# Where a run-time branch stands in the start of an attention and mixer kernel, and which queue issues the first loads

## The chip, the cores and the metric

One core of a Trainium2 chip. The time is device time in microseconds (us) of that core, given as the median of several runs. A profile is one execution of the program taken by the hardware profiler; its times count from the start of its span. The engines are TensorE (PE; its weight loads are PEld), VectorE (DVE), ScalarE (ACT), GpSimd (POOL) and SyncE (SP). SP computes nothing: it issues DMAs. ACT and POOL can issue DMAs as well. A name with a q behind it (SPq, DVEq) is an engine's sequencer, which handles register loads, branches and DMA issues.

## The reference

Attention with root-mean-square norm on Q and K, 8 batches of 12 heads, 448 tokens of 64 values, and then an MLP mixer over tokens and channels. All data is float32.

```python
q_n, k_n = (rmsnorm(q, g_q), rmsnorm(k, g_k))      # x / sqrt(mean(x*x) + 1e-6) * g
scores = scale * np.matmul(q_n, k_n.transpose(0, 1, 3, 2))
scores = scores - np.max(scores, axis=-1, keepdims=True)
attn = np.exp(scores)
attn = attn / (np.sum(attn, axis=-1, keepdims=True) + 1e-09)
attn_out = np.matmul(attn, v)                       # (8, 12, 448, 64)
x = attn_out.transpose(0, 2, 1, 3).reshape(8, 448, 768)
h = np.maximum(x.transpose(0, 2, 1) @ w_tok1, 0.0) @ w_tok2
u = x + h.transpose(0, 2, 1)
out = u + np.maximum(u @ w_ch1, 0.0) @ w_ch2
```

## The kernel before, in words

**The two arms.** The kernel decides at run time whether the exponentials need their row maximum taken off. From g_q and g_k it computes one flag, `large` (lines 1334 to 1337, four small DVE instructions). Line 1533 loads the flag into a register of every engine, and each engine branches by itself into one of two copies of `whole`: with `shifted` true the maximum is taken off, with `shifted` false it isn't. The profiled data goes to the second copy. An engine meets the branch where its own stream of instructions has it; nothing makes the engines branch together.

**What stands ahead of the branch.** The class `Start` (line 1299) issues the first loads and begins on the first heads. Heads are handled in pairs, 48 in all; pair 0 and 1 are heads 0 to 3 of batch 0. `load_qk(p)` (line 1390) takes the Q and K rows of a pair with four DMAs, two for Q and two for K, made by `loads` (line 1394, issued at line 1406) on the two queues that it is given. Ahead of the branch:

- SP issues Q of pairs 0 and 1, and then Q and K of pairs 2 and 3; ACT issues K of pairs 0 and 1.
- POOL issues four tiny loads of g (line 1341), makes the identity matrix and some constants, and has the small memset of `summand` (line 1379) for the two buffers of squares.
- ACT squares pairs 0 and 1 (`square`, line 1421, instructions of line 1429), in two halves each.
- DVE sums the squares (`reduce`, line 1435, instructions of line 1445), takes reciprocal square roots by a guess and three Newton steps (`roots`, `guess`, `newton`, lines 1448 to 1499) and scales the rows (`scale`, line 1490, instructions of line 1496). Between the two sums stands one small product on `g_t` (line 1365), which ACT uses later as the scale of a copy.

Then comes the branch, on DVE behind the scalings of pair 1 and on SP behind the last load of pair 3.

**What stands behind the branch.** `whole` (line 84) has its engine order written out by hand for TensorE, DVE, ACT and GpSimd. SP begins at line 1204: V of pairs 0 and 1 (`load_v`, line 404), and then in turn the weight chunks 0 to 4 (`weight_load`, line 205, DMAs of line 222), Q and K of pairs 4 and 5, and V of pairs 2 to 5. ACT squares pair 2 (line 1216), copies pair 0's transposed rows out of PSUM, squares pair 3 (line 1221) and copies pair 1's. PE transposes pairs 0 and 1 (`turn_qk`, line 419, transposes of line 429, copies of lines 435 and 437). DVE sums and roots pairs 2 and 3 and scales them (lines 1222 to 1228).

The steady part starts at line 1240: `att_items` gives the steps of attention and `weight_items` those of the weights, and `merge` interleaves both by estimated costs. In a step PE computes scores (line 455), ACT takes their exponential (line 459), and PE multiplies by V (line 528) and by ones for the row sums (line 508). In steps 1 and 2 of attention ACT squares pairs 4 and 5 between its exponentials; at the end of step 3 PE transposes pairs 2 and 3. Weights arrive as 64-bit numbers and are made float32 on the way: DVE's lines 345 to 350, ACT's line 356 and DVE's line 379. The tile `raw` that holds a chunk has five buffers, so load i + 2 waits for the last conversion of chunk i - 3. Score tiles and transposes share one pool of four PSUM buffers (`ps_S`).

Of the kernel before, what the change touches and what calls it, by code (L numbers as in the profile page):

```python
# [13 lines left out]
ALU = mybir.AluOpType  # L14
# [69 lines left out]
def whole(ctx, tc, shifted, pre, q, k, v, g_q, g_k, moe_w_tok1, moe_w_tok2, moe_w_ch1, moe_w_ch2, out):  # L84


    nc = tc.nc
# [3 lines left out]
    B, H, S, D = q.shape  # L91
# [58 lines left out]
    ws2 = dram.tile([P, NF9 * 8, P], F32, name="ws2")  # L150

    st = dict(pre.st)
    m_tile = lambda: ps_M.tile([P, 512], F32, name="m_ps", tag="M")
    s_tile = lambda name: ps_S.tile([P, 512], F32, name=name, tag="S")

# [43 lines left out]
    def columns(i):  # L199
        return WCOLS if chunks[i][2] is None else chunks[i][2].shape[-1]  # L200

    def raw_tile():
        return raw_pool.tile([P, WCOLS, 2], U32, name="raw")

    def weight_load(i):
        rows, srcs, dst = chunks[i]
        wide = srcs[0].dtype == I64
        t = raw_tile()
        flat = t[0:rows].rearrange("p n w -> p (n w)")
        if not wide:  # L210
            t = t[:].rearrange("p n w -> p (n w)").bitcast(F32)
            flat = t[0:rows]
        n = columns(i) // len(srcs) * (1 + wide)
        for k, src in enumerate(srcs):
            to = flat[:, k * n:(k + 1) * n]
            for a, part in enumerate(src if isinstance(src, tuple) else (src,)):
                at = to[a * D:(a + 1) * D] if isinstance(src, tuple) else to
                if wide:
                    part = part.bitcast(U32)
                if len(part.shape) == 3:  # L220
                    at = at.rearrange("p (i n) -> p i n", i=part.shape[1])
                nc.sync.dma_start(out=at, in_=part)
        st["raw", i] = t
# [177 lines left out]
    def heads(p):  # L401
        return pre.heads(p)

    def load_v(p):
        b, hs = heads(p)
        st["v", p] = vt = pre.v_0 if p == 0 else st["v45"][:, p - 4, :] if p in (4, 5) else pre.v_t[p % 3]
        for a in range(2):
            nc.sync.dma_start(
                out=vt[rows_of(p, a)].rearrange("r (k d) -> r k d", d=D),
                in_=v[b, hs][a].rearrange("(k r) d -> r k d", r=D))  # L410

    def rows_of(p, a):

        return slice((a ^ p % 2) * D, (a ^ p % 2) * D + D)
# [788 lines left out]

    load_v(0)
    load_v(1)
    for i in range(5):
        weight_load(i)
        if i < 2:
            pre.load_qk(4 + i, st)
            load_v(2 + i)  # L1210

    st["v45"] = tu_pool.tile([P, 2, S], F32, name="v45", tag="tu")
# [86 lines left out]
class Start:  # L1299


    def __init__(self, ctx, tc, q, k, g_q, g_k, w2, g2, gate):
        self.nc = nc = tc.nc
        self.q, self.k = q, k
        B, H, S, D = q.shape
        self.NPAIR, self.NS, self.D = H // 2, 4, D
        self.R = S // self.NS
        P = 128
        pool = lambda name, bufs: ctx.enter_context(tc.tile_pool(name=name, bufs=bufs))
        const = pool("start", 1)  # L1310
        KF = w2.shape[0] // P // 2
        self.hb = const.tile([P, HB, 4, S // 2], F32, name="hb")

        flat = self.hb[:].rearrange("p q f s -> p (q f s)")
        n, o = 4 * self.NS * D, self.NPAIR * 4 * self.NS * D
        self.st = {("qk", p): flat[:, p * n:(p + 1) * n] for p in range(self.NPAIR)}
        self.qkT = [flat[:, o + i * 2 * S:o + (i + 1) * 2 * S].rearrange("p (i s) -> p i s", i=2) for i in range(3)]
        assert flat.shape[-1] >= o + 3 * 2 * S
        self.v_0 = const.tile([P, S], F32, name="v_first")[:]
        self.first_slot = self.NPAIR  # L1320
        self.far = 3 * self.NPAIR + 2
        qk_t = const.tile([P, 2, n], F32, name="qk_t")
        self.qk_t = [qk_t[:, i, :] for i in range(2)]
        self.v_t = [const.tile([P, S], F32, name=f"v_{i}")[:] for i in range(3)]

        warm = const.tile([P, 1], F32, name="warm")
        nc.vector.memset(warm[:], 1.0)
        self.load_qk(0, self.st, other=nc.scalar)
        self.load_qk(1, self.st, other=nc.scalar)
        nc.scalar.activation(out=warm[:], in_=warm[:], func=AF.Square)  # L1330
        gg = gate.tile([1, D], F32, name="gg")
        most = gate.tile([1, 1], F32, name="most")
        self.large = large = gate.tile([1, 1], I32, name="large")
        nc.vector.tensor_tensor(out=gg[:], in0=g2[:, 0, :], in1=g2[:, 1, :], op=ALU.mult)
        nc.vector.tensor_tensor(out=gg[:], in0=gg[:], in1=gg[:], op=ALU.mult)
        nc.vector.tensor_reduce(out=most[:], in_=gg[:], axis=AX_X, op=ALU.max)
        nc.vector.tensor_scalar(large[:], most[:], SCORE_BOUND**2 / D, None, ALU.is_gt)
        self.g_t = const.tile([P, 2], F32, name="g_t")
        for i, g in enumerate((g_q, g_k)):
            for a in range(2):  # L1340
                nc.gpsimd.dma_start(
                    out=self.g_t[a * D:(a + 1) * D, i:i + 1], in_=g.rearrange("(p o) -> p o", o=1))
        self.ident = const.tile([P, P], F32, name="ident")
        make_identity(nc, self.ident[:, :])
        self.one_c = const.tile([P, D], F32, name="one_c")
        nc.gpsimd.memset(self.one_c[:], 1.0)
        self.expo_c = const.tile([P, 1], F32, name="expo_c")
        nc.gpsimd.memset(self.expo_c[:], -896.0 * 2**23)
        self.sq = const.tile([P, 4 * self.NS, D + 1], F32, name="sq")


        self.sq_2 = flat[:, 0:4 * self.NS * (D + 1)].rearrange("p (r d) -> p r d", d=D + 1)
        self.sq_1 = qk_t[:].rearrange("p i n -> p (i n)")[:, 0:4 * self.NS * (D + 1)].rearrange(
            "p (r d) -> p r d", d=D + 1)
        for sq in (self.sq, self.sq_1):
            self.summand(sq)
        self.load_qk(2, self.st)
        self.load_qk(3, self.st)
        self.rs_0 = const.tile([P, 8 * self.NS], F32, name="rs_0")
        with tc.tile_pool(name="st_0", bufs=1) as self.st_pool:  # L1360
            self.nt_pool = self.st_pool
            for p in range(2):
                self.square(p, self.st)
            self.reduce(0, self.st)
            nc.vector.scalar_tensor_tensor(
                out=self.g_t[:, 0:1], in0=self.g_t[:, 0:1], scalar=float(D) ** 0.5, in1=self.g_t[:, 1:2],
                op0=ALU.mult, op1=ALU.mult)
            self.reduce(1, self.st)
            for part in self.roots(0, self.st):
                part()  # L1370
            for p in range(2):
                self.scale(p, self.st)

    def heads(self, p):
        b, j = divmod(p, self.NPAIR)
# [130 lines left out]
def kernel(  # L1506
# [26 lines left out]
    with tc.If(nc.values_load(large[0:1, 0:1], min_val=0, max_val=1,  # L1533
                              skip_runtime_bounds_check_because="a comparison's result") > 0) as arm:
        whole(tc, True, pre, *args)
    with arm.Else():
        whole(tc, False, pre, *args)
# [30 lines left out]
```

## Time and profile before

| | |
|---|---|
| median of 3 runs | 1285.12 us (1283.40 to 1287.99) |
| the profiled execution | 1283.78 us |
| its span | 1282.0 us |
| PE busy | 1251.6 us |
| DVE, ACT, POOL busy | 795.3, 393.3, 387.9 us |
| first transposes on PE | 12.77 us after the start |
| SP's last load ahead of the branch ends | 9.97 us |
| SP's first load behind the branch begins | 13.41 us |
| DMA, mean over the span | 178 GB/s |

The page first gives the busy time of each engine. A timeline line has start, duration, engine, source line, operation, what it writes and reads, and in square brackets how long the engine stood idle before it and what it waited for. A line of the view of waits has the instruction, the thing it waited for, the total in us, how often, and the longest. The DMA queues are q1 (SP), q10 (ACT), q0 (GpSimd) and two queues that carry instructions, q8 and q14.

### The profile page before, as it was taken

To read this page: it belongs to the slowest core of one execution; us is meant where nothing else is said; L and a number is where in the kernel's file an instruction comes from. 1 tells how busy PE (TensorE), PEld (TensorE's weight loads), DVE (VectorE), ACT (ScalarE), POOL (GpSimd) and SP (SyncE) were. 2 spreads that over 40 slices of the span, in tenths; PEclk is the share of its full clock that TensorE was granted. 3 is DMA by queue.
4 is the path that set the end of the run, shared out by engine and by line. 5 is a ranking of instruction groups with operands and counts; after the bars stand their busy time and mean duration, and the time that the engine had idled before them with its cause. 6 is when DMAs were issued, how large, how long until landed. Compare 5 with 4: busy or idle time off the path is not lost.

```text
span 1282.0 us, 20022 instructions
## 1 busy us (share of the span) xinstructions
PE 1251.6 (98%) x7236; PEld 890.8 (69%) x7236; DVE 795.3 (62%) x1241; ACT 393.3 (31%) x785; POOL 387.9 (30%) x629
## 2 busy tenths in 40 slices
PE   4999999999999999999999999999999999999998
PEld 3444444457744487796778768885887867797998
DVE  6989778856664255864668356765558456554243
ACT  5663433223341144302443033311343024300210
POOL 1202552024995611331133122241122322131222
PEclk9999999999999999999999999999999999999999
DMA  7866595899899876695657867595766864386554
GB/s 174 192 188 175 154 233 147 208 241 250 239 237 229 195 165 169 142 249 117 159 161 160 207 142 185 131 222 123 190 159 141 236 134 138 115 208 146 185 175 103
DMA packets 490112, 228.37 MB, mean 178 GB/s; under 512 B 371860, under 2 KB 450580, under 8 KB 490004
## 3 DMA queue, kind: packets, MB, share of 16 engines
q1 hardware_dynamic: 483394, 214.25, 67.9%
q0 software_dynamic: 3584, 12.06, 3.1%
q8 instruction: 59, 0.97, 0.3%
q10 hardware_dynamic: 3026, 0.69, 0.3%
q14 instruction: 49, 0.40, 0.1%
HBM read 184.26 MB, written 42.66 MB: 177 GB/s over the span
## 4 chain that ended last, share of the span: by engine, by line
PE 86%; DVE 6%; DMA 2%; SPq 2%; issue 1%; ACT 1%; DVEq 0%; ACTq 0%
PE m_ps L1001 26%; PE m_ps L1067 21%; PE s_ps L455 9%; PE o_ps L528 8%; PE m_ps L881 5%; PE m_ps L971 5%; PE m_ps L1050 4%; PE m_ps L839 2%; PE t_ps L839 2%; PE d_ps L508 1%; DVE raw L346 1%; DVE raw L348 1%; DVE stage L379 1%; DMA raw<-wp 1%; PE m_ps L846 1%
## 5 line engine op out<-in xcount | busy, mean ns | idle before, releaser
L1067 PE MATMUL m_ps<-hb,unit 128*128 128x224 f32 x1440 | 277.2, 354 | 0.0
L1067 PEld LDWEIGHTS m_ps<-hb,unit 128*128 128x128 f32 x1440 | 270.9, 190 | 8.8 <-issue 7.7
L1001 PE MATMUL m_ps<-tu,unit 128*128 128x224 f32 x1008 | 201.6, 355 | 1.3 <-ACT r L1011 1.3
L1001 PEld LDWEIGHTS m_ps<-tu,unit 128*128 128x128 f32 x1008 | 189.1, 190 | 15.1 <-issue 9.2
L459 ACT ACTIVATE e<-s_ps 128x448 f32<-128x448 f32 x294 | 138.1, 549 | 177.7 <-PE s_ps L455 169.4
L1001 PE MATMUL m_ps<-uT,unit 128*128 128x224 f32 x756 | 151.2, 354 | 0.5 <-DVE hb L1007 0.5
L1001 PEld LDWEIGHTS m_ps<-uT,unit 128*128 128x128 f32 x756 | 142.2, 190 | 7.6 <-issue 4.6
L455 PE MATMUL s_ps<-qkT 64*64 64x448 f32 x1260 | 143.7, 545 | 0.8 <-ACT x L821 0.8
L528 PE MATMUL o_ps<-e,v 64*64 64x448 f32 x1148 | 129.4, 538 | 0.3 <-ACT uT L565 0.2
L496 DVE TENSOR_TENSOR es<-es,e 128x896 f32<-128x896 f32 x90 | 103.5, 1150 | 13.0 <-ACT e L459 7.6
L1007 DVE TENSOR_TENSOR hb<-m_ps,r 128x448 f32<-128x448 f32 x63 | 39.1, 621 | 108.5 <-POOL r L1007 57.0
L1007 POOL TENSOR_TENSOR hb<-r,r 128x448 f32<-128x448 f32 x21 | 24.0, 1143 | 243.6 <-ACT r L1023 243.6
L455 PEld LDWEIGHTS s_ps<-qkT 64*64 64x64 f32 x1260 | 44.9, 132 | 70.0 <-issue 59.9
L528 PEld LDWEIGHTS o_ps<-e,v 64*64 64x64 f32 x1148 | 45.2, 133 | 62.9 <-issue 59.2
L1475 POOL TENSOR_TENSOR nt<-rs 128x56 f32<-128x56 f32 (+1 forms) x54 | 21.9, 405 | 203.5 <-DVE rs L1467 200.7
L1008 ACT ACTIVATE hb<-hb 128x448 f32<-128x448 f32 x84 | 48.4, 577 | 101.1 <-DVE hb L1007 77.6
L881 PE MATMUL m_ps<-w_sb,h 128*128 128x448 f32 x192 | 75.2, 544 | 0.3 <-DVE uT L886 0.3
L1082 POOL TENSOR_TENSOR uT<-uT,r 128x448 f32<-128x448 f32 x42 | 51.4, 1240 | 78.5 <-DVE r L1082 46.7
L320 POOL TENSOR_TENSOR raw<-raw 128x128 f32<-128x128 f32 x128 | 64.4, 522 | 34.3 <-DMA raw<-wp 29.8
L1445 DVE TENSOR_REDUCE ms<-sq 128x28 f32<-128x896 f32 (+2 forms) x44 | 47.5, 1080 | 35.6 <-ACT sq L1432 28.6
L1007 DVE TENSOR_TENSOR r<-m_ps,r 128x448 f32<-128x448 f32 x42 | 26.1, 622 | 64.3 <-PE m_ps L1001 64.3
L886 DVE TENSOR_TENSOR uT<-uT,m_ps 128x448 f32<-128x448 f32 x48 | 29.3, 613 | 54.5 <-PE m_ps L881 54.5
(146 smaller groups left out, 1600.2 us busy)
## 6 DMA issues: line engine op xcount, KB each, us to landing
unit<-ws SPq DMA_DIRECT2D x267, 384.0 KB, 4.2
raw<-in_moe_w_ch_dram SPq DMA_DIRECT2D x72, 256.0 KB, 3.4
v<-in_v_dram SPq DMA_DIRECT2D x96, 112.0 KB, 3.9
out_dram<-turned SPq DMA_DIRECT2D x182, 56.0 KB, 1.9
xs<-xt SPq DMA_DIRECT2D x56, 168.0 KB, 4.7
qk_t<-in_q_dram SPq DMA_DIRECT2D x144, 56.0 KB, 3.5
qk_t<-in_k_dram SPq DMA_DIRECT2D x144, 56.0 KB, 3.7
x<-xs SPq DMA_DIRECT2D x42, 192.0 KB, 3.9
```

Source lines behind the costliest of these rows:

```text
L320: nc.gpsimd.tensor_tensor(out=at[o], in0=at[x], in1=at[y], op=ALU.add if op == "+" else ALU.subtract)
L455: nc.tensor.matmul(out=pss[i][rows_of(i, a), 0:S], lhsT=qkT[h, 1, k * D:(k + 1) * D], rhs=qkT[h, 0, :], start=True, stop=True)
L459: nc.scalar.activation(out=e[:, i, :], in_=pss[i][:, 0:S], func=AF.Exp)
L496: nc.vector.tensor_tensor(out=es[:], in0=(es if k > 1 else st["e", t, 0])[:], in1=st["e", t, k][:], op=ALU.add)
L528: nc.tensor.matmul(out=st["o", p][a * D:(a + 1) * D, 0:S], lhsT=vt[rows, k * D:(k + 1) * D], rhs=e[rows, :], **kw)
L839: nc.tensor.matmul(out=st["t1", h][jc][:, 0:HC], lhsT=w1_sb[:, c, jc * P:(jc + 1) * P], rhs=st["x", b, h][:, :, c, :], start=start and c = ...
L881: nc.tensor.matmul(out=ps[:, 0:S], lhsT=st["h1", jc][:, cc * P:(cc + 1) * P], rhs=w2_sb[:, jc].rearrange("p c r -> p (c r)"), start=(jc == ...
L971: nc.tensor.matmul(out=ps, lhsT=a[:, o + 2 * half, :], rhs=natural(half * KF + t) if wide else u[:, half * KC + t, :], start=(t == 0 and h ...
L1001: nc.tensor.matmul(out=ps[:, j * HS:(j + 1) * HS], lhsT=w[:, t, j, :], rhs=m, start=(t == 0), stop=(t == KC - 1))
L1007: add = lambda e, o, x, y: e.tensor_tensor(out=o, in0=x, in1=y, op=ALU.add)
L1067: nc.tensor.matmul(out=ps[:, x * HS:(x + 1) * HS], lhsT=st["w"][:, tile_at % 6, :], rhs=hb[:, X_SLOT[f], i, :], start=(i == 0), stop=(i == 3))
L1082: e.tensor_tensor(out=get(out), in0=get(x_), in1=get(y), op=ALU.add if op == "+" else ALU.subtract)
```

## The change

Four things change. DVE's sums, roots and scalings of pairs 0 and 1 and the product on `g_t` move out of `Start` into a new method, `first_pairs`, which `whole` calls in both arms; so DVE's branch comes right behind the four instructions that make the flag, and the `g_t` product comes after pair 0's scaling instead of between the sums. The Q and K loads of pairs 2 and 3 go from SP to GpSimd, behind its memsets; so SP's branch comes behind the Q loads of pairs 0 and 1. The first loads behind SP's branch are in another order: Q and K of pair 4 ahead of weight chunk 0, and Q and K of pair 5 ahead of V of pair 2. And the small tiles of sums and roots of pairs 0 and 1 come from the pools of `whole` instead of a pool of their own.

```diff
@@ whole
     st = dict(pre.st)
+    pre.first_pairs(st)
...
     load_v(0)
     load_v(1)
+    pre.load_qk(4, st)
     for i in range(5):
         weight_load(i)
+        if i == 0:
+            pre.load_qk(5, st)
         if i < 2:
-            pre.load_qk(4 + i, st)
             load_v(2 + i)
@@ Start.__init__
         for sq in (self.sq, self.sq_1):
             self.summand(sq)
-        self.load_qk(2, self.st)
-        self.load_qk(3, self.st)
+        for p in (2, 3):
+            for part in self.loads(p, self.st, nc.gpsimd, nc.gpsimd):
+                part()
         self.rs_0 = const.tile([P, 8 * self.NS], F32, name="rs_0")
-        with tc.tile_pool(name="st_0", bufs=1) as self.st_pool:
-            self.nt_pool = self.st_pool
-            for p in range(2):
-                self.square(p, self.st)
-            self.reduce(0, self.st)
-            nc.vector.scalar_tensor_tensor(
-                out=self.g_t[:, 0:1], in0=self.g_t[:, 0:1], scalar=float(D) ** 0.5, in1=self.g_t[:, 1:2],
-                op0=ALU.mult, op1=ALU.mult)
-            self.reduce(1, self.st)
-            for part in self.roots(0, self.st):
-                part()
-            for p in range(2):
-                self.scale(p, self.st)
+        for p in range(2):
+            self.square(p, self.st)
+
+    def first_pairs(self, st):
+
+        D = self.D
+        self.reduce(0, st)
+        self.reduce(1, st)
+        for part in self.roots(0, st):
+            part()
+        self.scale(0, st)
+        self.nc.vector.scalar_tensor_tensor(
+            out=self.g_t[:, 0:1], in0=self.g_t[:, 0:1], scalar=float(D) ** 0.5, in1=self.g_t[:, 1:2],
+            op0=ALU.mult, op1=ALU.mult)
+        self.scale(1, st)
```

## The prediction

> **What bounds the kernel now.** I read the page's head first: TensorE (PE) is busy almost throughout, so only its idle time can be won, and all its idle time is 1282.0 - 1251.6 = 30.4 us. The view of waits on PE says where it lies.
>
> ```profile
> PE 1251.6 (98%) x7236; PEld 890.8 (69%) x7236; DVE 795.3 (62%) x1241; ACT 393.3 (31%) x785; POOL 387.9 (30%) x629
> ```
>
> ```profile
> PE t_ps L429 <- DVE hb L1496: 12.8, 1, 12.8
> PE t_ps L429 <- ACT e L459: 3.5, 2, 3.3
> PE t_ps L846 <- DMA x<-xs: 2.7, 1, 2.7
> ```
>
> Columns: us in total, times, longest. The change touches the first two: the start, before the first transposes, and one gap of 3.3 us. The third, at 430 us, hangs on work that is not edited. Next the timeline of the first 32 us:
>
> ```profile
> 11.37 1.06 ACT L1429 ACTIVATE sq<-hb 112x1024 f32<-112x1024 f32 x1 [2.67 <-DVE rs L1488]
> ...
> 13.41 1.46 SPq L408 DMA_DIRECT2D v_first<-in_v_dram  x2
> ...
> 15.99 1.24 DVE L1445 TENSOR_REDUCE ms<-sq 112x16 f32<-112x1040 f32 x1 [1.63 <-ACT hb L435]
> ...
> 24.32 1.06 ACT L1429 ACTIVATE sq<-hb 112x1024 f32<-112x1024 f32 x1 [3.71 <-DMA hb<-in_k_dram]
> ...
> 27.39 0.43 DVE L345 TENSOR_SCALAR cv_sb<-raw 128x512 uint32<-128x512 uint32 x1 [2.08 <-DMA raw<-in_moe_w_tok_dram]
> ...
> 29.23 1.06 ACT L1429 ACTIVATE hb<-hb 112x1024 f32<-112x1024 f32 x1 [2.11 <-DMA hb<-in_k_dram]
> ...
> 31.41 0.82 PE L429 MATMUL t_ps<-ident,hb 112*128 112x112 f32 x3 [3.27 <-ACT e L459]
> ```
>
> ScalarE (ACT) stands 3.71 us before the squares of pair 4 and 2.11 us before those of pair 5, each time for a K load; the exponentials behind the second square hold the score buffers, so PE stands 3.27 us. Those loads are late because SyncE (SP) issues nothing between 9.97 and 13.41 us: it is in its branch. The record of the branch line, start in us at the end:
>
> ```profile
> L1533 PEldq COMPARE_BRANCH  x1: 5624/5624/5624, 3.7 to 3.7; - x1
> ...
> L1533 ACTq COMPARE_BRANCH  x1: 45/45/45, 8.4 to 8.4; - x1
> ...
> L1533 SPq COMPARE_BRANCH  x1: 45/45/45, 10.6 to 10.6; - x1
> ...
> L1533 DVEq TENSOR_LOAD <-large x1: 540/540/540, 12.2 to 12.2; - x1
> L1533 DVEq COMPARE_BRANCH  x1: 67/67/67, 12.8 to 12.8; - x1
> ```
>
> From branch to first instruction behind it: ACT 8.4 to 11.37, 3.0 us; SP 10.6 to 13.41, 2.8 us; VectorE (DVE) 12.8 to 15.99, 3.2 us, of which 1.62 us show (its last scaling ends at 14.37). PE, which branches at 3.7 us, takes 5.6 us. The view by stretches tells how full the transfers are then (last two columns: DMA share and GB/s):
>
> ```profile
> 4.00:7.00 3.00, 0.00 (x0) 0.00 (x0) 0.99 (x2) 2.04 (x4) 0.37 (x5) 1.00 1.10 216
> ...
> 11.00:15.00 4.00, 2.23 (x12) 2.26 (x13) 3.23 (x8) 2.05 (x3) 0.00 (x0) 1.00 0.20 41
> ```
>
> **What the Trainium skill says.** "Runtime: NRT & Kernel Launch", Instruction fetch mechanics: a taken branch whose target isn't on chip waits for a DMA that fetches it. The trace agrees: the DMA view has instruction packets between 6 and 7 us (after PE's and GpSimd's branch at 3.7 and 4.4) and between 13.4 and 14.4 (after DVE's). The fetch came 2.5 us after the branch with the transfers full, 1.0 us after it with them empty. "TensorE: Matmul & The Clock Gate", What's actually happening: after some 3.4 us of idleness PE runs at half clock. It agrees: in the stretch 32 to 34 us the granted clock is 0.50, and the 16 transposes there take 3.25 us against 1.75 us at 52.86. "SBUF — State Buffer", Who interferes with whom: a DMA that GpSimd issues can be held up by a DVE instruction, but not by tensor_reduce, which is what DVE runs here. "DMA: Bandwidth & Descriptors", Queues, rings and completion order: each DMA engine takes turns between queues, packet by packet. It agrees: from 4.5 to 6 us SP's queue moved 0.17 MB and ACT's 0.15 MB.
>
> **The change, part by part.**
>
> (a) *DVE's branch comes forward* from 12.8 to about 3.7 us (large is ready at 3.03, register load 0.54). Removed: the 1.62 us at 14.37. Added: everything that DVE does for pairs 0 and 1 waits for the fetch. Bounds: 3.2 us as at 12.8, so DVE works from 6.9; or PE's 5.6 us, so 9.3. I take 8.5: fetching now coincides with full transfers, as PE's did, but PE's packet is 1.35 us long and the other engines' about 0.55, 0.8 less. The four half sums at 0.66 us each and the last at 0.69 then end at 11.2 instead of 9.58: the first transposes start **1.6 us later** (0 at 6.9, since the last square ends at 8.71; 2.4 at 9.3). The small product for g_t (0.16 us) moves behind scale(0), beside PE's transposes: nothing. It waited for g_t's loads to 8.14; that wait is covered now.
>
> (b) *SP's branch comes forward.* After the four Q loads of pairs 0 and 1 (issued by 3.1) it branches at 3.7; by the same fetch its first V load is issued at about 8.2 (6.5 to 9) instead of 13.41. All that SP issues behind comes some 5 us earlier, as far as the DMA engines let it: they gain the 3.5 us that stood nearly empty (11.5 to 15).
>
> (c) *Loads of pairs 2 and 3 on GpSimd.* Eight DMAs behind its memsets, from 4.4. The nearest rows of its DMAs:
>
> ```profile
> 145.80 0.81 POOL L266 DMA_DIRECT2D few<-ws  x1 [0.24 <-issue]
> ...
> 154.56 0.75 POOL L266 DMA_DIRECT2D few<-ws  x1 [2.27 <-DMA ws<-few]
> ```
>
> These have 512 pieces, ours 448; I take 0.8 us. Eight end at 10.8, and with 3.7 us from issue to landing (DMA view, same row) pair 2's last lands at 10.5, pair 3's at 13.7; shared with SP's V loads some 15.5. SP issued the same by 9.97. ACT wants them when the copies of pair 0 and 1 leave room: 11.4 to 12.7, and 15.07 + 1.6 = 16.7. So nothing, with 1 us to spare; what it costs without that cover is the slow rival below. GpSimd's own branch moves to 11; its next work is a memset at 15.49 and roots at 37: nothing.
>
> (d) *Order on SP.* Pair 4 goes ahead of weight chunk 0; pair 5 ahead of V of pair 2 and chunk 1. Pair 4 is there at about 17 and pair 5 at 22, where ACT will ask at 22.2 and 25.1 (its times of before, 20.62 and 23.5 without the two waits, plus 1.6). Both waits go. Chunk 1 comes after 15 DMAs instead of 11: 8.2 + 15 x 0.7 = 18.7, landing near 25; DVE asks for it at 25.8 instead of standing to 27.39.
>
> *The sum.* Without the two ACT waits PE's scores of 25.88 start at 25.5, when its own values end, and take 1.5 us; the transposes follow at 27.05 instead of 31.41: 4.36 us. With no gap the clock stays up and they take 1.6 us instead of 3.25: 1.6 us more. So 5.96 us, less the head's 1.6: **4.4 us** at 34.66. What is late next: DVE, which is full from 28 to 79 us, gains 27.39 - 25.8 = 1.6 us there and the two waits for PE and ACT at 40.87 and 43.70 (0.99 + 0.63): 3.2 us. Its scaling of pair 5, done at 50.67, would be done at 47.5, and PE asks for it at 52.86 - 4.4 = 48.5: enough. At 82 us DVE still stood 2.83 us for PE, so the difference of 1.2 does no harm. ACT's weight step at 50.5 comes 0.2 to 0.3 us late in a stretch where ACT is full: **net 4.1 us**. Later chains (194 to 250, 400 to 430 us) begin and end on PE and shift along. The profiled execution took 1283.78 us (span 1282.0 and 1.78 around it), 1.3 below the median of the runs; 1283.78 - 4.1 = 1279.7, and against the median 1285.12 - 4.1 = **1281.0**, which I forecast.
>
> **The rivals.**
>
> *The fetches are quick*, as ACT's at 8.4 was with transfers at 187 GB/s. Then DVE starts at 6.9, the head loses nothing, and 5.96 less some 0.3 gives 1285.1 - 5.7 = 1279.4. Against it: PE's 5.6 us at just the moment in question.
>
> *The gain is taken back*: PE comes early to something that doesn't. For it: transfers at share 1.18 from 30 to 46 us, and from 194 to 250 us a chain over DVE and weight transfers. If those keep their times, the wait there grows by what was won and 0.5 us is left: 1284.6. Against: each link of that chain was released by the one before, back to PE at 192.8.
>
> *GpSimd's loads are late, and the kernel slower.* Place: ACT's square of pair 3, ahead of the copies of pair 1 in ACT's order, so PE's first scores wait. At c us per DMA pair 3 lands at 4.4 + 8c + 2.9; from 16.7 on every us counts in full, and 4.1 us are gone at c = 1.7. The skill's SBUF page, in "A bandwidth-pool intuition that's wrong", has such a DMA go from 620 to 3100 ns beside a DVE copy, an upper bound that the row of 0.75 to 0.81 doesn't support; at c = 2.4 pair 3 lands at 26.5 and the time is 1281.0 + 9.8 = 1290.8. If the head alone is later than I think, 2.4 for 1.6, 1281.8 comes out, still a gain.
>
> **How the numbers follow.** Forecast 0.55 (1281.0, its own range 1279.5 to 1282.6 by the head's 0 to 2.4 with the cases apart); quick fetch 0.17 (1279.4); taken back 0.16 (1284.6); GpSimd late 0.08 (1290.8); not listed 0.04, half of it slower. This kernel's measurement can tell about 0.3%, 3.9 us, from no change: faster means under 1281.3. Of the forecast somewhat over half lies there, with nearly all of the quick fetch: 0.48. Slower: 0.08 + 0.02 = 0.10. The rest 0.42. The range goes from 1278.0, below the quick fetch, to 1286.0, past the case taken back; it leaves out the slow case and tails.
>
> **What would show it.** (a) branch records of DVE and SP at 3.7; DVE's first sum at 8.5 (6.9 to 9.3); first transposes at 14.4. (b) SP's first V load at 8.2 and no stretch with DMA share 0.20. (c) GpSimd's DMAs 0.8 us each, ACT's square of pair 3 without a wait for DMA. (d) no waits of ACT for K loads of pairs 4 and 5, PE's second transposes near 28.7 and at full clock, 1.6 us. Wrong it would be if ACT waits for pair 3, or if PE's waits after 40 us grow by more than 1 us.

## The result, and the profile after

The changed kernel takes 1280.12 us in the median of 20 runs (1276.77 to 1283.99), the kernel before 1285.59 us (1280.32 to 1287.99). The two medians lie 5.5 us apart; the ratio over all runs, by which this text goes, is 0.9964 with a 95% interval of 0.9955 to 0.9973: 4.6 us less, 3.5 to 5.8 by the interval. The profiled execution took 1280.59 us with a span of 1278.8; that is 3.2 us less than the profiled one before.

Page and waits on PE, changed kernel (total in us, times, longest):

```profile
PE 1249.1 (98%) x7236; PEld 887.4 (69%) x7236; DVE 796.8 (62%) x1241; ACT 393.6 (31%) x785; POOL 394.8 (31%) x637
```

```profile
PE t_ps L430 <- DVE hb L1502: 14.4, 1, 14.4
PE t_ps L847 <- DMA x<-xs: 5.2, 1, 5.2
...
PE t_ps L430 <- ACT e L460: 0.3, 1, 0.3
```

The gap of 3.3 us ahead of the second transposes is 0.3. The wait at the start grew from 12.8 to 14.4. The wait for x, at 427 us, grew from 2.7 to 5.2, which the forecast did not have. Timeline of the changed kernel (line numbers are a few higher than before: 1435 squares, 1451 sums, 430 transposes, 1412 Q and K loads):

```profile
4.29 1.46 POOL L1412 DMA_DIRECT2D hb<-in_q_dram  x2
...
8.76 1.30 DVE L1451 TENSOR_REDUCE ms<-sq 112x8 f32<-112x520 f32 x2 [5.73 <-ACT qk_t L1435]
9.04 3.17 SPq L409 DMA_DIRECT2D v_first<-in_v_dram  x2
...
12.60 1.06 ACT L1435 ACTIVATE sq<-hb 112x1024 f32<-112x1024 f32 x1 [3.46 <-DVE nt L1493]
...
14.45 3.22 PE L430 MATMUL t_ps<-ident,hb 112*128 112x112 f32 x16 [14.45 <-DVE hb L1502]
...
21.96 1.09 ACT L1435 ACTIVATE sq<-hb 112x1024 f32<-112x1024 f32 x1
...
25.01 1.07 ACT L1435 ACTIVATE hb<-hb 112x1024 f32<-112x1024 f32 x1
...
27.22 0.43 DVE L346 TENSOR_SCALAR cv_sb<-raw 128x512 uint32<-128x512 uint32 x1 [0.79 <-DMA raw<-in_moe_w_tok_dram]
...
28.84 1.75 PE L430 MATMUL t_ps<-ident,hb 112*128 112x112 f32 x16
```

Read it against the lines of before. The squares of pairs 4 and 5 (21.96 and 25.01) carry no bracket: ACT no longer stands for their K. The second transposes start at 28.84 instead of 31.41 and take 1.75 us instead of 3.25. The price is in the lines at 8.76 and 14.45. The 5.73 us in brackets are put down to ACT, whose squares of pair 0 were done by 6.4; what DVE stood for is its branch. DVE and SP now branch at 3.7 us, as PE does, and their first instructions behind it are those at 8.76 and 9.04. The record of the branch line:

```profile
L1539 PEldq COMPARE_BRANCH  x1: 5444/5444/5444, 3.7 to 3.7; - x1
L1539 DVEq COMPARE_BRANCH  x1: 67/67/67, 3.7 to 3.7; - x1
L1539 SPq COMPARE_BRANCH  x1: 45/45/45, 3.7 to 3.7; - x1
```

And by stretches, the one that was nearly empty before (DMA share 0.20, 41 GB/s):

```profile
11.00:15.00 4.00, 0.55 (x3) 0.58 (x4) 3.62 (x15) 1.06 (x1) 0.00 (x0) 1.00 0.62 140
```

PE runs the same work in the same order in both kernels, so the same instruction can be looked up in both timelines:

| on PE | before | after | earlier by |
|---|---|---|---|
| first transposes | 12.77 | 14.45 | -1.7 |
| second transposes, begin | 31.41 | 28.84 | 2.6 |
| values behind them | 34.59 | 30.52 | 4.1 |
| a weight product in line 971 | 250.36 | 246.02 | 4.3 |
| a product in line 1001 | 335.28 | 329.97 | 5.3 |
| transposes behind the wait for x | 429.84 | 427.07 | 2.8 |
| end of the span | 1282.0 | 1278.8 | 3.2 |

What the change aims at, 4.1 us, is won before 35 us, and 3.7 of it still stand at 200 us. Between 200 and 335 us this profile wins 1.6 us more, of which some 1.1 are shorter waits of PE, and in one wait at 427 us it loses 2.5. In the other nine profiles of this document the lead changes by -1.1 to +0.2 us from 200 to 335 us, so that win belongs to this execution.

### The profile page after: what moved, and what is told of

It is laid out like the page before. It is cut to its first block, busy times and chain, and to the rows that moved or that the text cites. A ratio compares the mean times of both kernels' runs of the same rounds, so it can differ in the third digit from the quotient of the medians.

```text
span 1278.8 us, 20023 instructions
## 1 busy us (share of the span) xinstructions
PE 1249.1 (98%) x7236; PEld 887.4 (69%) x7236; DVE 796.8 (62%) x1241; ACT 393.6 (31%) x785; POOL 394.8 (31%) x637
## 4 chain that ended last, share of the span: by engine, by line
PE 88%; DVE 5%; DMA 2%; SPq 1%; ACT 1%; issue 1%; DVEq 0%; ACTq 0%
PE m_ps L1002 25%; PE m_ps L1068 22%; PE s_ps L456 9%; PE o_ps L529 9%; PE m_ps L882 6%; PE m_ps L972 5%; PE m_ps L1051 4%; PE m_ps L840 2%; PE t_ps L840 2%; PE d_ps L509 1%; PE m_ps L509 1%; DVE es L497 1%; DVE raw L349 1%; DVE raw L347 1%; PE t_ps L430 1%
```

## The experiments

Theory A, from the prediction: time is won where ACT no longer waits for K of pairs 4 and 5, because SP starts 4 to 5 us earlier or asks for these loads sooner; DVE's early branch costs the head what it gives back later. Rival B: DVE's early branch pays. All ratios are against the kernel before, on the same chip.

**Only DVE's branch early**: the changed kernel with the parts of SP and GpSimd undone.

```diff
-        for p in (2, 3):
-            for part in self.loads(p, self.st, nc.gpsimd, nc.gpsimd):
-                part()
+        self.load_qk(2, self.st)
+        self.load_qk(3, self.st)
...
-    pre.load_qk(4, st)
     for i in range(5):
         weight_load(i)
-        if i == 0:
-            pre.load_qk(5, st)
         if i < 2:
+            pre.load_qk(4 + i, st)
             load_v(2 + i)
```

> Only VectorE's branch is moved; SyncE issues the loads of pairs 2 and 3 ahead of its branch and the old order follows. A: first transposes at 14.4, ScalarE still waits for K of pairs 4 and 5 (5.8 us in all less the 1.7 us that it comes later), second transposes at 31.4 as before, time within 1 us of 1285.6. B: a gain of 2 us or more.

Measured: 1283.87 us, ratio 0.9992 (0.9977 to 1.0007), no change shown. First transposes at 14.78, second at 32.17. Waits on ACT up to 60 us:

```profile
ACT hb L1432 <- DMA hb<-in_k_dram: 2.9, 1, 2.9
ACT sq L1432 <- DMA hb<-in_k_dram: 1.8, 1, 1.8
```

The two K waits stand (2.9 for pair 5 and 1.8 for pair 4, against 2.11 and 3.71), so the gap on PE stands, 2.9 us. B falls as an explanation of the whole gain: the interval leaves DVE's branch at most 3.0 of the 4.6 us, and the kernels below that have the gain with DVE late show that it isn't needed.

**Only the order of loads new**: the kernel before with these lines.

```diff
+    pre.load_qk(4, st)
     for i in range(5):
         weight_load(i)
+        if i == 0:
+            pre.load_qk(5, st)
         if i < 2:
-            pre.load_qk(4 + i, st)
             load_v(2 + i)
```

> Only the order of SyncE's loads behind its branch is new (pair 4 ahead of weight chunk 0, pair 5 ahead of V of pair 2); all branches stand as before. A: K of pair 5 lands near 25.5 instead of 29.1, ScalarE's waits shrink from 5.8 to about 2 us, second transposes near 28.3 at full clock, time near 1281.5. B: without early branches no gain, 1285.6.

Measured: 1282.39 us, ratio 0.9981 (0.9970 to 0.9992), 2.4 us. Second transposes at 28.92, near the expected 28.3, and PE 3.8 us ahead of the kernel before at 35 us; ACT's two K waits were 1.2 and 1.9 us. But at 52 us nothing of it is left in the profile, and this profiled execution was the slowest of the 22 (1285.18 us), so it can't show how the median gained. Waits on DVE up to 60 us, and on PE:

```profile
DVE cv_sb L345 <- DMA raw<-in_moe_w_tok_dram: 4.8, 2, 3.0
```

```profile
PE m_ps L508 <- DVE dt L557: 2.3, 1, 2.3
```

Asking for K sooner on a queue that is itself late makes the weight chunks later. DVE stood 2.08 us for one of them before and 4.8 us now; it then reads PE's row sums late, and PE waits 2.3 us for a buffer, at 43.6 us. Behind that its clock is 0.50 for 3.4 us. In this execution the wait moved from ACT to DVE and from there back to PE. The expectation had the first half of this and not the second.

**SP early, GpSimd's loads and the new order; DVE as before**: the changed kernel with DVE's sums, roots and scalings back in front of the branch. Against the kernel before it has the new order of loads, as in the experiment above, and these lines:

```diff
-        self.load_qk(2, self.st)
-        self.load_qk(3, self.st)
+        for p in (2, 3):
+            for part in self.loads(p, self.st, nc.gpsimd, nc.gpsimd):
+                part()
```

> SyncE's early branch, GpSimd's loads and the new order are kept; VectorE's sums, roots and scalings of pairs 0 and 1 stay ahead of its branch, as before. Theory A (the time is won where ScalarE no longer waits for the K loads of pairs 4 and 5; VectorE's early branch costs 1.7 us at the head and only gives VectorE's own 1.6 us back): first transposes at 12.8 us again, second transposes at 27.1 instead of 28.8, time 1280.0 or lower; VectorE's branch at 12.8 now fetches beside running transfers and may come out at 17 instead of 16. Theory B (VectorE's early branch is what pays): second transposes no earlier than 28.8 and a time of 1283 or more.

Measured: 1277.39 us, ratio 0.9943 (0.9921 to 0.9966), in 6 runs. First transposes at 13.60 and second at 28.00, both 0.8 to 0.9 us later than expected and still earlier than in the changed kernel; PE 4.9 us ahead at 35 us (4.1 in the changed kernel). Because few runs stood behind this, it was run once more:

> The kernel with SyncE early, GpSimd's loads and the new order, VectorE as before, once more, beside the changed kernel on one chip: 1277 to 1279 and 1.5 to 3 us under the changed kernel, if VectorE's early branch costs; equal to it within 1 us, if the first result was chance.

Measured: 1279.32 us, ratio 0.9963 (0.9948 to 0.9978); first transposes at 13.09, second at 27.54. The changed kernel took 1279.63 us beside it, so by the expectation the first result was chance: the times do not differ, though PE's start does.

**The changed kernel with the old order of loads**: the diff of the order experiment, reversed.

> The changed kernel with the old order of SyncE's loads. A with SyncE's early start alone enough: K of pair 4 lands near 20, of pair 5 near 25, ScalarE waits under 1 us, second transposes near 29, time within 1 us of the changed kernel's 1280.1 to 1281. If the order is what matters: ScalarE's waits come back with 2 us or more, second transposes near 31 and a time near 1284.

Measured: 1278.94 us, ratio 0.9957 (0.9943 to 0.9972). Second transposes at 29.35. ACT waits once, for K of pair 5:

```profile
ACT hb L1433 <- DMA hb<-in_k_dram: 1.8, 1, 1.8
```

More than the expected 1 us, but PE stands only 0.5 us for it and the total is not shown to be worse. The new order is not needed.

**SP early and GpSimd's loads alone**: DVE as before, old order.

```diff
-        self.load_qk(2, self.st)
-        self.load_qk(3, self.st)
+        for p in (2, 3):
+            for part in self.loads(p, self.st, nc.gpsimd, nc.gpsimd):
+                part()
```

> SyncE's early branch with pairs 2 and 3 on GpSimd alone; VectorE stays as before and so does the order of loads. A (SyncE's early start is what pays, VectorE's early branch costs head, order adds nothing): first transposes near 13.2 us, second near 28.5, time 1278 to 1279.5, with the kernel that adds the new order to it within 1 us. If the new order matters once VectorE is late: 1281 or more.

Measured: 1280.21 us, ratio 0.9967 (0.9957 to 0.9977). First transposes at 12.95, second at 28.35. SP's first V load, and the stretch that was nearly empty:

```profile
8.27 1.46 SPq L408 DMA_DIRECT2D v_first<-in_v_dram  x2
```

```profile
11.00:15.00 4.00, 2.05 (x11) 2.08 (x12) 3.37 (x9) 1.88 (x3) 0.00 (x0) 1.00 1.00 172
```

The time is 0.7 us above A's range and 0.8 us below that of its rival; it is 0.9 us above that of the kernel with the new order. By the ratios these three lines do the whole of the change. One K wait stays, 2.5 us for pair 5, of which 0.9 us show on PE.

**The changed kernel once more**, beside the last ones.

> The changed kernel itself, for a second profile and times on the same chip: 0.996 of the kernel before; second transposes at 28.8 us again. If the 5.2 us wait for the transfer of x at 427 us is chance, it is between 1.4 and 3 us here, as in the other profiles; if it belongs to the change it is near 5 again.

Measured: 1279.63 us, ratio 0.9954 (0.9937 to 0.9972). The profile differs in two places above all (timeline and waits):

```profile
9.76 1.29 DVE L1451 TENSOR_REDUCE ms<-sq 112x8 f32<-112x520 f32 x2 [6.73 <-ACT qk_t L1435]
```

```profile
PE t_ps L847 <- DMA x<-xs: 0.9, 1, 0.9
```

DVE came out of its branch 1.0 us later than in the first profile, and PE's first and second transposes followed at 15.45 and 30.61, so the expected 28.8 did not come again. The wait for x was 0.9 instead of 5.2. Over the eleven profiles of this document, whose kernels share this later part, it was between 0.9 and 5.2, with no order by kernel. So the 2.5 us that the first profile lost there are the spread from one execution to the next, not a cost of the change.

**Fewer loads in flight at the branch**: the changed kernel with pair 1 on GpSimd too.

```diff
-        self.load_qk(1, self.st, other=nc.scalar)
...
-        for p in (2, 3):
+        for p in (1, 2, 3):
```

> The changed kernel with the loads of pair 1 on GpSimd as well, behind its memsets, so that between the branches at 3.7 us and 6.5 us only half as much is in flight. If the fetch is slow because the transfers are full: VectorE's first sum at 7 us or before instead of 8.8 and SyncE's first V load at 6.5 to 7.5 instead of 9.0. If the fetch at that moment is slow for another reason: both as in the changed kernel. The time itself may go either way, since pair 1 arrives later.

Measured: 1284.68 us in one run. Timeline, the branch line of PE, and the stretch behind the branches (DMA share 0.43; 1.06 in the changed kernel):

```profile
7.07 1.52 SPq L409 DMA_DIRECT2D v_first<-in_v_dram  x2
7.22 1.29 DVE L1450 TENSOR_REDUCE ms<-sq 112x8 f32<-112x520 f32 x2 [4.20 <-ACT sq L1434]
```

```profile
L1538 PEldq COMPARE_BRANCH  x1: 4144/4144/4144, 3.7 to 3.7; - x1
```

```profile
4.00:7.00 3.00, 0.00 (x0) 0.00 (x0) 0.00 (x0) 1.15 (x2) 3.00 (x9) 1.00 0.43 101
```

All three come out sooner: SP at 7.07 (9.04 and 8.03 in the two profiles of the changed kernel), DVE at 7.22 (8.76 and 9.76), PE after 4.1 us (5.4 and 6.2). The branches were at the same 3.6 to 3.7 us, and what differs at that moment is how many loads are in flight: these slow the fetch. The trace's records of DMA packets say the same. The first packet of instructions behind the branches starts at 4.85 us here and at 6.35 and 6.23 us in the two profiles of the changed kernel. From that packet to the first instruction on SP and DVE it is 2.2 and 2.4 us here and 1.8 to 3.5 us there, so only the way to the packet is shorter. That three engines fetch at once is not the reason: they do so here too, and in the kernel before, where SP and DVE branch later, PE's branch took 5.6 us. The single run lies above all 28 of the changed kernel (up to 1283.99 us): pair 1 arrives late, and PE is 5.7 us behind the kernel before at 26 us.

**SP early without GpSimd**: the changed kernel, but SP issues pairs 2 and 3 itself, behind its branch; the loads of V of pairs 0 and 1 come behind these.

```diff
+    pre.load_qk(2, st)
+    pre.load_qk(3, st)
...
-        for p in (2, 3):
-            for part in self.loads(p, self.st, nc.gpsimd, nc.gpsimd):
-                part()
```

> The changed kernel without GpSimd's part: SyncE branches at once and issues the loads of pairs 2 and 3 itself, as the first ones behind its branch, ahead of V of pairs 0 and 1. If GpSimd's taking these eight loads is what lets SyncE's early branch pay: pair 3 lands near 16 to 18 us, V of pair 0 is issued near 13.5 as in the kernel before, ScalarE stands for pair 2 or 3 and again for K of pair 5, second transposes at 31 or later, time 1284 to 1287. If SyncE's early branch is enough by itself: 1280 to 1281.

Measured: 1281.07 us, ratio 0.9973 (0.9963 to 0.9983), 3.5 us. The stretches, and ACT's waits:

```profile
7.00:11.00 4.00, 0.00 (x0) 0.00 (x0) 1.42 (x3) 1.28 (x3) 0.00 (x0) 1.00 0.20 43
```

```profile
ACT sq L1434 <- DMA hb<-in_k_dram: 6.0, 1, 6.0
```

The empty stretch is back, only earlier: SP's first load behind its branch is issued at 9.47 us, the transfers are nearly idle from 7 to 11 us, and ACT stands 6.0 us for K of pair 2. V of pair 0 is issued at 15.59, later than in the kernel before. Yet the time is 3.5 us better and the loss that was expected did not come. Its profiled execution was the slowest of its runs (1285.97 us): PE is 2.3 us ahead at 35 us and 0.1 us at 52.8, and DVE stands 3.2 us for a weight chunk on the way. Where the gain of the other runs lies is taken up below the next table. By the ratios GpSimd's part is worth some 1.5 us, the difference between 0.9973 and about 0.996, and the intervals overlap.

Together, as ratios:

| | SP late | SP early, pairs 2 and 3 on GpSimd |
|---|---|---|
| DVE late, old order | 1 | 0.9967 |
| DVE late, new order | 0.9981 | 0.9943, 0.9963 |
| DVE early, old order | 0.9992 | 0.9957 |
| DVE early, new order | not run | 0.9964, 0.9954 |

The right column is flat within its intervals of 0.0009 to 0.0023 to each side. No version is shown to beat the changed kernel; those with DVE late start PE 0.9 to 2.5 us sooner in their profiles, and a difference of 1 us in the total could not be told apart here.

**What of the gain is clock.** Each run on record has the mean clock that TensorE was granted. In the profiles it is 0.50 in single stretches of 3.4 us or twice that and at the very end, and 1.00 elsewhere. One such stretch of 3.4 us takes 0.0013 off the mean of a run and, by estimate, costs a full PE half of it, 1.7 us. The profiles of the three kernels with SP late have one early, from 31.2 us (before), 33.0 us (only DVE early) and 44.7 us (only the order new), each near a wait of PE of 2.3 to 3.3 us. Of the eight profiles with SP early seven have none before 424 us; that of the kernel with pair 1 on GpSimd has one from 23.1 us, behind a wait of 2.3 us. Behind the wait for x some profiles have a stretch and some have none, which is part of the spread between runs. Mean times of the runs whose clock is on record, sorted by it (number of runs in brackets; the third column takes the six entries on the right of the table above together):

| clock of the run | before | SP early, pairs 2 and 3 on GpSimd | SP early without GpSimd |
|---|---|---|---|
| 0.997 | 1283.8 (46) | 1281.5 (25) | 1283.3 (5) |
| 0.998 | 1281.9 (15) | 1279.4 (22) | 1281.4 (4) |
| 0.999 | 1280.3 (2) | 1278.4 (18) | 1280.8 (6) |
| mean clock | 0.9964 (102) | 0.9982 (79) | 0.9985 (22) |

At one clock SP's early branch with GpSimd's loads gains some 2 us; the rest of the gain, about half, goes with the higher clock, and 0.0018 of 1280 us is indeed 2.3 us. Without GpSimd hardly anything is gained at one clock, and nearly the whole gain goes with the clock. The groups are small and were sorted afterwards, so this is a reading of the record and not an experiment. Why that kernel's loads, late as they are, spare PE the early stretch is only in part shown: PE's longest wait ahead of its second transposes is 0.4 us in its profile.

## Why the prediction was right, step by step

Forecast 1281.0, measured 1280.12; a gain of 4.1 us forecast, 4.6 (3.5 to 5.8) measured.

- **DVE's branch** (a). First sum at 8.5 forecast, 8.76 and 9.76 in two profiles; first transposes at 14.4, measured 14.45 and 15.45. Taking PE's slow branch as the nearest row, because it fell into the same moment, was right, and the experiment with fewer loads shows its reason. Taking 0.8 us off it for a shorter packet was not borne out: the five profiles with DVE early and eight loads in flight have the first sum between 8.67 and 9.76, around 9.2, and PE's row alone gave 9.3. The value that DVE's own record of before gave, 6.9, would have been 2 to 3 us off.
- **SP's branch** (b). First V load at 8.2 forecast, 9.04 and 8.03 measured. The share of 0.20 between 11 and 15 us became 0.62. The experiments confirm that this is the part that pays.
- **GpSimd's loads** (c). 0.8 us each forecast; eight took 5.65 us, 0.71 each. ACT's square of pair 3 had no wait. Pair 2 was squared at 12.60, 1.2 us later than before, right behind ACT's own branch, and still ahead of the copies of pair 0 at 15.46. The slow rival, GpSimd late, is refuted: it began at 1.7 us per DMA. That DVE's sums do not hold these DMAs up agrees with the runs: with DVE late its sums run beside most of them, and each still took 0.71 us.
- **The order** (d). Both ACT waits went, as forecast. That the order was needed for it was not claimed in so many words, but the working gave the landing times with both edits in place. With the old order one wait goes too and the one for pair 5 stays (1.8 and 2.5 us), of which PE feels 0.5 and 1.2.
- **The sum.** Second transposes at 28.65 by the working (27.05 + 1.6), measured 28.84; they took 1.75 us where 1.6 was put. PE's lead behind them: 4.4 forecast, 4.1 measured, 2.3 in the second profile, in which DVE's fetch took 1 us more. The close agreement of the first profile is in part luck: the scores ahead of the transposes began at 26.50 instead of 27.1 and took 2.3 us instead of 1.5, two errors that cancel. The term for the clock, 1.6 us, is well borne out: no profile of the changed kernel has the early stretch at 0.50, and the runs' mean clock is higher. Only its condition was too strict: the prediction says some 3.4 us of idleness, and here waits of 3.3, 2.9 and 2.3 us were enough.
- **What is late next.** This step was off. DVE was to gain 3.2 us by 43.7 us; it gained 1.95 (its line of 43.70 stands at 41.75). Chunk 1 landed at 27.2 and not at 25, so DVE won 0.2 us there instead of 1.6: SP began 0.8 us later than put and took 0.8 us per DMA instead of 0.7, so the chunk was issued at 20.98 and not at 18.7. ACT's weight step at 50.5, which was to be 0.2 to 0.3 us late, stood 1.0 us for DVE, and PE's lead fell from 4.1 to 3.7. The sum came out because DVE's slack just sufficed: it had pair 5 scaled at 48.76 us and PE asked for it at 48.91, 0.15 us where the working had 1.0.
- **Later chains shift along.** In the first profile they did, and won 1.6 us more, up to 427 us, where the wait for x took 2.5 us. With that a sign that the prediction had set for being wrong, PE's waits after 40 us growing by more than 1 us, was met in the first profile (some 9.1 to 10.4 us) and not in the second (7.6 us); the spread over eleven profiles shows it as chance. The rival "taken back" is refuted: PE's lead lasts past the chain from 194 to 250 us in both profiles (4.3 and 2.5 us there), and the time is won.
- **The total.** 4.1 us forecast and 4.6 measured is closer than the account by profiles warrants: the two profiles of the changed kernel end 3.2 and 1.5 us before that of the kernel before. The mechanism is shown by the experiments, the agreement to half a microsecond is not.

## What to carry to other kernels

A run-time branch costs its engine a fetch, and what that costs in all depends on which engine stands: on the engine that issues the loads it leaves the DMA engines empty, so let that engine branch early and give another queue the loads that must be in flight meanwhile. On an engine whose results come first, branching early moves the same fetch into the moment when the transfers are fullest; here no gain from it was shown. Before moving a load ahead in a late queue, ask what stands behind it: in its profile the order alone moved the wait from the K loads to the weights. And before reading a difference of a few microseconds off one profile, look at where the granted clock fell in it and in the other runs: a short wait of TensorE can cost its own length and a slow stretch behind it.

## What the runs showed of the hardware

The fetch behind a taken branch is no constant. From branch to first instruction it took 2.7 to 3.0 us on SP at 10.6 to 11.2 us with the transfers draining, 4.3 to 5.8 us on SP and 5.0 to 6.1 us on DVE at 3.7 us with them full, and 3.4 to 3.5 us at 3.7 us with half the loads in flight. Between two profiles of one and the same kernel DVE's differed by 1.0 us. With the transfers full the first packet of instructions starts 2.5 to 3.0 us after the branches, with half the loads in flight 1.2 us after them; the first instructions on SP and DVE come some 2 to 3.5 us behind that packet. The eight loads on GpSimd moved as few, large packets: between 8 and 9.4 us its queue moved 0.28 MB in 115 packets, where SP's queue of before moved 0.22 MB in 870 for the same kind of load. In the first 60 us TensorE's clock fell to 0.50 for 3.4 us in four of the eleven profiles, each time at or within 1.2 us of the end of a wait of 2.3 to 3.3 us.
